# The folded weight W' as three products of rounded terms, and the second batch's turned probabilities copied by ACT

## The chip, the cores and the metric

The kernel runs on one core of a Trainium2 chip. The metric is the device time in microseconds (us) of one execution. PE is the matrix engine, PEld its weight load, DVE the vector engine, ACT the scalar engine, POOL the GpSimd engine, SP the queue that issues most transfers. Each engine works through its own list of instructions in order and waits on semaphores for the others.

## The reference

Three layers follow one another on 2 batches of 768 tokens.

```python
x = attention(q, k, v)                  # 8 heads of 64, a window of 96 and 8 global keys
for e in range(4):                      # attention experts, top 2 of 4 by a gate
    a = softmax(mask(scale * (x @ wq[e]) @ (x @ wk[e]).T))
    ye = a @ (x @ wv[e]) @ wo[e]
    out += gate[:, e] * ye
u = out + transposed(transposed(out) @ U @ V)
y = u + relu(u @ w_ch1) @ w_ch2         # 512 -> 2048 -> 512
```

The kernel never forms `ye` at full width before the first channel product. It keeps the gated expert outputs z (256 wide, 4 experts of 64) and multiplies the stacked `wo` (256x512) into `w_ch1` (512x2048) once: W' = wo @ w_ch1, 256x2048. That product is what the change touches.

## The kernel before, in words

The first part works on 24 pairs of softmax rows: pairs 0 to 11 belong to the first layer, 12 to 17 to the expert attention of batch 0, 18 to 23 to that of batch 1. The code runs over positions; position r computes the scores of pair r + 1 (L485, into PSUM tiles S), the values of pair r - 1 (L774) and the transposes ("turns", L442) of pair r. A pair's way is: PE scores, DVE minima with the mask (L489), ACT exponentials (L500), DVE reciprocal sums (L507 to L510, `rec`), POOL normalisation of the probabilities `pr` (L513), PE transposes into PSUM banks T and U, a copy of each bank to SBUF (`pt`, in `moved`, L289 on ACT for even groups and L292 on DVE for odd ones), PE values. A pair of batch 1 has 3 or 4 groups.

Free room in a position is filled with other products. W' is folded there in 8 slices of 256 columns (`w_fold`): f = 0 in position 15, 1 in 17, 2 in 18, 3 to 5 in 19 to 21, half of 6 in 22; slice 7 and the other half of 6 follow in the tail, behind the last scores. Each slice is 2 row halves times 4 contraction blocks, in plain fp32, which the chip runs as two instructions each: 16 instructions. The slice of `w_ch1` arrives as 64-bit numbers; `w_load` loads it (two raw tiles `cr`), `narrow_sign` (ACT L303, POOL L304) and `narrow_join` (DVE L309, L310) make fp32 tiles `ct` of 128x512 from it, one position ahead of the fold. The result in PSUM (`acc`) is split by `out` into a rounded term (ACT, `wph`) and the remainder (DVE L295, `wpl`), because the later products run on such pairs of terms: `three` multiplies high by high, low by high and high by low in the faster fp32r format (L631, L632). After the tail, the second part (`M`) computes the two channel products in 64 steps, all of it with `three`.

The order of the instructions on each engine is written by a planner (class `Order`) from costs of its own; on PE it keeps the order of the code, on the other engines it moves instructions freely within their dependences.

## Time and profile before

| what | us |
|---|---|
| median of 3 runs (445.39 to 447.91) | 445.65 |
| the profiled execution | 447.32 |
| its span in the profile | 445.2 |
| PE busy in it | 431.1 |
| DVE, ACT, POOL busy in it | 241.6, 194.5, 115.0 |

A busy time says how long an engine was at work, not that it set the end. The span is what the profile covers; 2.1 us of the execution lie outside it. In timelines an instruction's length includes the part that overlaps the next one on the same engine, so what an instruction costs is read from the distance between starts.

### The profile page before, as it was taken

The page shows a single profiled execution, that of the slowest core. Times are in us where ns is not written, and L with a number is a line of the kernel's source. Part 1 is how long each engine was busy: PE and PEld are TensorE (multiplying, and loading weights), DVE is VectorE, ACT ScalarE, POOL GpSimd, SP SyncE. Part 2 cuts the span into 40 slices and gives each one's busy share as a digit, 9 for nine tenths or more (in the row PEclk, how much of TensorE's full clock was granted, in tenths as well). Part 3 has the DMA queues.
Part 4 walks back from the last instruction along what each step waited for, and adds up shares of the span by engine and source line. Part 5 has one row for each costly group of instructions (what it writes and reads, how often), then busy time and mean ns, then how long its engine had stood idle before and what let it go on. Part 6 is the DMA issues. An engine that isn't in the chain of part 4 may idle for free.

```text
span 445.2 us, 9063 instructions
## 1 busy us (share of the span) xinstructions
PE 431.1 (97%) x3444; PEld 373.4 (84%) x3444; DVE 241.6 (54%) x726; ACT 194.5 (44%) x539; POOL 115.0 (26%) x211
## 2 busy tenths in 40 slices
PE   6999999999999999999999999999999999999993
PEld 4777899888888987788888888888888888899993
DVE  6888757885656876987897995111121212221211
ACT  5788676666455556575654652111111111111111
POOL 7756556326232434445221230000000000000000
PEclk9999999999999999999999999999999999999998
DMA  7888853006303123333353422000020000200002
GB/s 262 277 268 274 280 170 77 2 1 237 97 1 96 51 92 113 122 100 104 116 160 112 144 76 73 1 1 0 1 71 0 1 0 1 71 1 0 1 0 78
DMA packets 21733, 39.34 MB, mean 88 GB/s; under 512 B 2802, under 2 KB 7922, under 8 KB 21682
## 3 DMA queue, kind: packets, MB, share of 16 engines
q1 hardware_dynamic: 19952, 37.11, 26.1%
q10 hardware_dynamic: 1730, 1.57, 1.0%
q8 instruction: 29, 0.48, 0.4%
q14 instruction: 22, 0.18, 0.1%
HBM read 35.53 MB, written 3.15 MB: 87 GB/s over the span
## 4 chain that ended last, share of the span: by engine, by line
PE 52%; ACT 0%; ACTq 0%; DVE 0%; issue 0%; DVEq 0%
PE h L631 10%; PE acd L631 8%; PE h L632 5%; PE acc L631 5%; PE X L631 4%; PE acd L632 4%; PE T L631 4%; PE U L631 3%; PE acc L632 2%; PE X L632 2%; PE T L632 2%; PE U L632 1%; PE acc L848 1%; PE S L631 0%; PE X L774 0%; PE T L874 0%
## 5 line engine op out<-in xcount | busy, mean ns | idle before, releaser
L930 DVE SCALAR_TENSOR_TENSOR pr<-h,pr 128x384 fp32r<-128x384 f32 x64 | 35.7, 557 | 133.0 <-ACT pr L929 132.9
L513 POOL TENSOR_SCALAR pr<-pr,rec 128x192 f32<-128x192 f32 (+5 forms) x144 | 76.0, 547 | 96.4 <-DVE rec L510 54.0
L929 ACT ACTIVATE pr<-h 128x384 fp32r<-128x384 f32 x64 | 31.5, 492 | 141.4 <-PE h L632 141.3
L500 ACT ACTIVATE pr<-pr,nm 128x192 f32<-128x192 f32 (+5 forms) x144 | 73.2, 513 | 25.2 <-DVE nm L489 21.0
L304 POOL TENSOR_SCALAR cr<-cr 128x512 f32<-128x512 f32 (+2 forms) x35 | 27.3, 785 | 50.3 <-ACT ct L303 27.0
L848 PE MATMUL acc<-ct,woT 128*128 128x256 f32 x128 | 29.4, 380 | 0.0
L489 DVE CUSTOM_DVE_ANT_0 pr<-S,zT 128x192 f32<-128x192 f32 (+1 forms) x96 | 27.4, 339 | 1.6 <-PE S L541 1.3
L310 DVE SCALAR_TENSOR_TENSOR ct<-ct,cr 128x512 int32<-128x512 int32 (+2 forms) x35 | 27.2, 776 | 0.9
L500 ACT ACTIVATION_READ_ACCUMULATOR pr<-pr,nm 128x1 f32 x144 | 27.5, 191 | 0.0
L489 DVE CUSTOM_DVE_ANT_0 pr<-S,cm 128x512 f32<-128x512 f32 (+3 forms) x48 | 24.7, 552 | 4.2 <-PE S L485 4.0
L309 DVE SCALAR_TENSOR_TENSOR cr<-cr 128x512 int32<-128x512 int32 (+2 forms) x35 | 24.6, 704 | 2.7 <-POOL cr L304 2.6
L848 PEld LDWEIGHTS acc<-ct,woT 128*128 128x128 f32 x128 | 23.5, 190 | 3.0 <-DVE zT L906 0.2
L442 PE MATMUL T<-ident,pr 128*128 128x128 f32 x144 | 24.2, 278 | 1.6 <-POOL pr L513 0.9
L632 PE MATMUL acd<-w2h,pr 128*128 128x512 f32 x64 | 25.4, 396 | 0.0
L631 PE MATMUL acd<-w2l,pr 128*128 128x512 f32 x64 | 25.3, 396 | 0.0
L631 PE MATMUL acd<-w2h,pr 128*128 128x512 f32 x64 | 25.3, 395 | 0.0
L303 ACT ACTIVATE ct<-cr 128x512 f32<-128x512 f32 (+2 forms) x35 | 22.6, 651 | 5.9 <-PE acc L848 5.9
L442 PE MATMUL U<-ident,pr 128*128 128x128 f32 x136 | 23.3, 278 | 0.3
L541 PE MATMUL S<-qk 64*64 64x192 f32 (+1 forms) x384 | 20.0, 346 | 2.3 <-DMA qk<-in_qk_dram 1.7
L485 PE MATMUL S<-qk,qk 64*128 64x512 f32 (+3 forms) x128 | 21.4, 462 | 0.0
L774 PEld LDWEIGHTS X<-pt,v 128*64 128x64 f32 x336 | 18.1, 137 | 3.5 <-issue 2.0
L292 DVE COPY pt<-T 128x384 f32<-128x384 f32 (+1 forms) x26 | 15.8, 608 | 9.6 <-PE T L442 9.3
(290 smaller groups left out, 1043.8 us busy)
## 6 DMA issues: line engine op xcount, KB each, us to landing
cr<-in_w_dram SPq DMA_DIRECT2D x32, 512.0 KB, 3.6
v<-in_vt_dram SPq DMA_DIRECT2D x32, 256.0 KB, 3.9
qk<-in_qk_dram SPq DMA_DIRECT2D x8, 320.0 KB, 3.8
qk<-in_qk_dram SPq DMA_DIRECT2D x8, 272.0 KB, 3.7
qk<-in_qk_dram SPq DMA_DIRECT2D x8, 256.0 KB, 4.2
out_dram<-o SPq DMA_DIRECT2D x12, 128.0 KB, 1.8
out_dram<-o ACTq DMA_DIRECT2D x12, 128.0 KB, 1.9
...
```

The source lines that it names most:

```text
L304: nc.gpsimd.tensor_scalar(hi.bitcast(F32), hi.bitcast(F32), 0.0, -0.0, op0=ALU.mult, op1=ALU.add)
L309: nc.vector.scalar_tensor_tensor(lo, lo, 29, hi, op0=ALU.logical_shift_right, op1=ALU.bitwise_or)
L310: nc.vector.scalar_tensor_tensor(t, t, 3, lo, op0=ALU.logical_shift_left, op1=ALU.bitwise_or)
L442: self.nc.tensor.transpose(t[:, k * P : (k + 1) * P], s, self.ident)
L489: self.nc.vector.tensor_tensor_reduce(out=out, in0=sp, in1=mask, scale=scale, scalar=start, op0=ALU.add, op1=ALU.min, accum_out=nm)
L500: self.nc.scalar.activation(pr[:, h, :], pr[:, h, :], AF.Exp, bias=nm[h], scale=-1.0, accum_out=den[:, k, h : h + 1])
L513: nc.gpsimd.tensor_scalar(pr[:, h, :], pr[:, h, :], rec[:, k - k0, h : h + 1], 0.0, op0=ALU.mult, op1=ALU.add)
L631: mm(out, lh, rh, start=first, stop=False), mm(out, lh, rl, start=False, stop=False),
L632: mm(out, ll, rh, start=False, stop=last)]
L848: nc.tensor.matmul(ac[:, n, :], self.woT[:, kc, p * P : (p + 1) * P], w1[kc // 2][:, kc % 2, :], start=kc == 0, stop=kc == 3)
L929: nc.scalar.activation(hh, hp, AF.Relu)
L930: nc.vector.scalar_tensor_tensor(hl, hp, 0.0, hh.bitcast(F32), op0=ALU.max, op1=ALU.subtract)
```

## The change

W' is folded by `three`. For that `woT` (the transposed `wo`) is loaded into a raw tile instead of a tile of its own, and split by POOL into `woTh` and by DVE into `woTl` (128x1024 each, once). Each `ct` tile is split too: for a slice's first tile ACT rounds, for its second POOL, and DVE subtracts for both (128x512 each). For slices 0 to 4 these terms lie in the columns of `wph` and `wpl` that slices 4 to 7 will fill later; for slices 5 to 7 in new tiles `c`, in a pool `wt2` that opens in position 20. A slice is then 24 fp32r instructions of 128x128 by 128x256. The second edit gives `moved` a flag: for batch 1 the odd groups are copied by ACT as well, 10 copies of 128x512 over positions 18 to 22 and the tail.

```diff
--- before.py
+++ after.py
@@ -441,9 +441,9 @@
         for k, s in enumerate(srcs):
             self.nc.tensor.transpose(t[:, k * P : (k + 1) * P], s, self.ident)
 
-    def moved(self, t, w, g):
+    def moved(self, t, w, g, late=False):
         pt = self.soft_.tile([P, 512], F32, tag=f"pt{g % 2}", name=self.uid("pt"), bufs=2)
-        (self.hi_dve if g % 2 else self.hi_act)(pt[:, :w], t[:, :w])
+        (self.hi_dve if g % 2 and not late else self.hi_act)(pt[:, :w], t[:, :w])
         return pt
 
 
@@ -762,7 +762,7 @@
             us = st["units"]
             t = self.ps("T")
             self.transposes(t, [us[k][0][:, h, kk * P : (kk + 1) * P] for k, kk in groups[g] for h in range(2)])
-            return lambda: st.__setitem__(g, self.moved(t, 2 * P * len(groups[g]), g))
+            return lambda: st.__setitem__(g, self.moved(t, 2 * P * len(groups[g]), g, b == 1))
 
         def values():
             v = self.st[b][2]
@@ -817,9 +817,24 @@
 
     def w_begin(self, wpool, tmp):
         self.wp = [wpool.tile([P, 2, DFF], F32R, name=f"wp{x}") for x in "hl"]
-        self.woT = tmp.tile([P, 4, 2 * P], F32, name="woT")
+        self.woT = [tmp.tile([P, 4, 2 * P], F32R, name=f"woT{x}") for x in "hl"]
         self.w1 = {}
-        self.nc.sync.dma_start(self.woT, self.a["woT"].rearrange("(c r) n -> r c n", r=P))
+
+    def wt_load(self):
+        r = self.raw_tile().bitcast(F32)[:, : 2 * DM].rearrange("p (c n) -> p c n", c=4)
+        self.nc.sync.dma_start(r, self.a["woT"].rearrange("(c r) n -> r c n", r=P))
+        yield
+        self.hi_pool(self.woT[0], r)
+        yield
+        self.lo_dve(self.woT[1], r, self.woT[0])
+        yield
+
+    def w_terms(self, f):
+
+        if f < 5:
+            return [[self.wp[x][:, :, n * CW : (n + 1) * CW] for x in range(2)] for n in ((7, 6) if f % 2 == 0 else (5, 4))]
+        made = [[self.wt2.tile([P, 2, CW], F32R, tag=f"c{x}{n}", name=self.uid("c"), bufs=2) for x in "hl"] for n in range(2)]
+        return made
 
     def w_load(self, f):
         raws, ts = [], []
@@ -830,12 +845,19 @@
             raws.append(raw.rearrange("p (n w) -> p n w", w=2))
         yield
         for r in raws:
-            ts.append(self.wtmp.tile([P, DM], I32, name=self.uid("ct")) if f > 5 else self.narrow_tile())
+            ts.append(self.narrow_tile())
             self.narrow_sign(r, ts[-1])
-        self.w1[f] = [t.bitcast(F32).rearrange("p (c n) -> p c n", c=2) for t in ts]
         yield
         for r, t in zip(raws, ts):
             self.narrow_join(r, t)
+        yield
+        self.w1[f] = terms = self.w_terms(f)
+        ts = [t.bitcast(F32).rearrange("p (c n) -> p c n", c=2) for t in ts]
+        for x, t in enumerate(ts):
+            [self.hi_act, self.hi_pool]["AP"[x] == "P"](terms[x][0], t)
+        yield
+        for t, (h, l) in zip(ts, terms):
+            self.lo_dve(l, t, h)
         yield
 
     def w_fold(self, f, ps=slice(0, 2)):
@@ -845,8 +867,8 @@
         ac = self.bank(self.side).rearrange("p (t n) -> p t n", t=2)[:, ps, :]
         for n, p in enumerate(range(2)[ps]):
             for kc in range(4):
-                nc.tensor.matmul(
-                    ac[:, n, :], self.woT[:, kc, p * P : (p + 1) * P], w1[kc // 2][:, kc % 2, :], start=kc == 0, stop=kc == 3)
+                wh, wl = [w[:, kc, p * P : (p + 1) * P] for w in self.woT]
+                self.three(ac[:, n, :], wh, wl, *[x[:, kc % 2, :] for x in w1[kc // 2]], kc == 0, kc == 3)
         fs = slice(f * CW, (f + 1) * CW)
 
         def out():
@@ -1172,7 +1194,8 @@
         at(11, "mid", self.gate, 0)
         at(17, "mid", self.gate, 1)
         for f, r in enumerate(folds):
-            stages(lambda f=f: self.w_load(f), (r - 2, "dma"), (r - 1, "sign"), (r - 1, "a"))
+            stages(lambda f=f: self.w_load(f), (r - 2, "dma"), (r - 1, "sign"), (r - 1, "a"), (r - 1, "mid"), (r - 1, "end"))
+        stages(self.wt_load, (13, "dma"), (14, "sign"), (14, "mid"))
 
         def middle():
             if not dense:
@@ -1188,6 +1211,7 @@
             self.close(x1p, wpl, stk0)
             self.w2a = self.open("w2a", "right")
             self.wo_tiles(self.w2a)
+            self.wt2 = self.open("wt2", "right")
             for b in range(B):
                 self.y_tiles(b, self.w2a)
 
@@ -1355,7 +1379,7 @@
         for e in ev[1]:
             e()
         do(r + 1, "end")
-        self.close(self.wtmp, self.s1p, self.psumR, self.psumS)
+        self.close(self.wt2, self.wtmp, self.s1p, self.psumR, self.psumS)
         self.psumS = self.open("psumS", space=PSUM)
         self.psumR = self.open("psumR", space=PSUM)
         self.pp = {"h": self.psumS, "acd": self.psumR}
```

On PE the rows of a slice are replaced where they stood, and nothing else moves. This is slice 3 in position 19, with the values of the pair before (X) and the first transposes (U and T are PSUM banks) ahead of it; of the slice's own rows, those of the first half stand here. Before:

```order
L774 MATMUL X_2759<-pt_2732,v_1980 64x128 x4
L774 MATMUL X_2759<-pt_2734,v_1980 64x128 x4
L442 MATMUL U_2809<-ident,pr_2651 128x128 x4
L442 MATMUL T_2814<-ident,pr_2651 128x128 x4
L848 MATMUL acc_2823<-ct_2667,woT 128x256 x2
L848 MATMUL acc_2823<-ct_2670,woT 128x256 x2
```

And now, down to the first contraction block of the slice:

```order
L774 MATMUL X_2827<-pt_2782,v_1980 64x128 x4
L774 MATMUL X_2827<-pt_2784,v_1980 64x128 x4
L442 MATMUL U_2877<-ident,pr_2699 128x128 x4
L442 MATMUL T_2882<-ident,pr_2699 128x128 x4
L631 MATMUL acc_2893<-wph,woTh 128x256
L631 MATMUL acc_2893<-wpl,woTh 128x256
L632 MATMUL acc_2893<-wph,woTl 128x256
```

A row of two instructions has become three rows, and so on for the 8 blocks of the slice: 24 instructions instead of 16.

On DVE the stretch from position 21 into 22 carries the end of pair 22, the term splits of slice 6 and the first minima of pair 23 (`nm`). Before, from the sign joins of slice 6 on:

```order
L309 SCALAR_TENSOR_TENSOR cr_2864<-cr_2864 128x512
L310 SCALAR_TENSOR_TENSOR ct_3011<-ct_3011,cr_2864 128x512
L507 TENSOR_SCALAR rec_3088<-den_2996 128x4
L508 RECIPROCAL rec_3088<-rec_3088 128x4
L510 TENSOR_TENSOR rec_3088<-rec_3088,g_1981 128x4
L292 COPY pt_3061<-U_3054 128x512
L295 TENSOR_TENSOR wpl<-acc_3038,wph 128x2x256
L309 SCALAR_TENSOR_TENSOR cr_2866<-cr_2866 128x512
L310 SCALAR_TENSOR_TENSOR ct_3014<-ct_3014,cr_2866 128x512
L489 ISA pr_3096,nm_3098<-S_3063,cm 128x512
L489 ISA nm_3098 128x1
L292 COPY pt_3133<-U_3126 128x512
```

And now:

```order
L309 SCALAR_TENSOR_TENSOR cr_2955<-cr_2955 128x512
L309 SCALAR_TENSOR_TENSOR cr_2957<-cr_2957 128x512
L310 SCALAR_TENSOR_TENSOR ct_3126<-ct_3126,cr_2955 128x512
L507 TENSOR_SCALAR rec_3227<-den_3111 128x4
L508 RECIPROCAL rec_3227<-rec_3227 128x4
L510 TENSOR_TENSOR rec_3227<-rec_3227,g_1981 128x4
L310 SCALAR_TENSOR_TENSOR ct_3129<-ct_3129,cr_2957 128x512
L295 TENSOR_TENSOR wpl<-acc_3159,wph 128x2x256
L295 TENSOR_TENSOR c_3154<-ct_3126,c_3153 128x512
L295 TENSOR_TENSOR c_3156<-ct_3129,c_3155 128x512
L489 ISA pr_3235,nm_3237<-S_3202,cm 128x512
L489 ISA nm_3237 128x1
```

The copies of `pt` are gone, both joins (L309 to L310) stand close together, and two subtractions of terms (`c`) stand between the remainder of slice 5 (`wpl`) and the first minimum.

On POOL, the stretch from pair 22's normalisation to pair 23's, before:

```order
L513 TENSOR_SCALAR pr_2995<-pr_2995,rec_3088 128x640 x2
L513 TENSOR_SCALAR pr_2995<-pr_2995,rec_3088 128x384 x2
L304 TENSOR_SCALAR cr_2962<-cr_2962 128x512
L304 TENSOR_SCALAR cr_2964<-cr_2964 128x512
L513 TENSOR_SCALAR pr_3096<-pr_3096,rec_3160 128x512 x2
L513 TENSOR_SCALAR pr_3096<-pr_3096,rec_3160 128x128 x2
```

And now:

```order
L513 TENSOR_SCALAR pr_3110<-pr_3110,rec_3227 128x640 x2
L286 TENSOR_SCALAR c_3155<-ct_3129 128x512
L513 TENSOR_SCALAR pr_3110<-pr_3110,rec_3227 128x384 x2
L304 TENSOR_SCALAR cr_3077<-cr_3077 128x512
L304 TENSOR_SCALAR cr_3079<-cr_3079 128x512
L513 TENSOR_SCALAR pr_3235<-pr_3235,rec_3315 128x512 x2
L286 TENSOR_SCALAR c_3276<-ct_3250 128x512
L513 TENSOR_SCALAR pr_3235<-pr_3235,rec_3315 128x128 x2
```

The rounding of slice 6's second tile (`c`, L286) stands between pair 22's two sizes, and that of slice 7's between pair 23's.

On ACT, position 22, where the exponentials of pair 23 (`pr`, L500) lie, before:

```order
L289 ACTIVATE pt_3059<-T_3049 128x512
L289 ACTIVATE wph<-acc_3038 128x2x256
L303 ACTIVATE ct_3111<-cr_2964 128x512
L289 ACTIVATE zT_99<-X_3071 128x2x128
L289 ACTIVATE pt_3131<-T_3121 128x512
L500 ACTIVATE pr_3096,den_3097<-pr_3096,nm_3098 128x512
L500 ACTIVATE pr_3096,den_3097<-pr_3096,nm_3100 128x512
L289 ACTIVATE pt_3152<-T_3142 128x512
L500 ACTIVATE pr_3096,den_3097<-pr_3096,nm_3102 128x128
L500 ACTIVATE pr_3096,den_3097<-pr_3096,nm_3104 128x128
L289 ACTIVATE wph<-acc_3135 128x256
```

And now:

```order
L289 ACTIVATE zT_99<-X_3210 128x2x128
L289 ACTIVATE pt_3270<-T_3260 128x512
L289 ACTIVATE pt_3272<-U_3265 128x512
L500 ACTIVATE pr_3235,den_3236<-pr_3235,nm_3237 128x512
L500 ACTIVATE pr_3235,den_3236<-pr_3235,nm_3241 128x128
L289 ACTIVATE pt_3305<-T_3295 128x512
L303 ACTIVATE ct_3250<-cr_3079 128x512
L289 ACTIVATE pt_3307<-U_3300 128x512
L500 ACTIVATE pr_3235,den_3236<-pr_3235,nm_3239 128x512
L500 ACTIVATE pr_3235,den_3236<-pr_3235,nm_3243 128x128
L289 ACTIVATE c_3274<-ct_3247 128x512
L289 ACTIVATE wph<-acc_3280 128x256
```

Four copies of `pt` stand there instead of two, and the second head's two exponentials come last, behind the third and fourth copy and a sign step of slice 7 (L303).

## Rows read from the trace of the kernel before

**Rows 1.** The page, first part: busy time, share and instructions of each engine.
```profile
PE 431.1 (97%) x3444; PEld 373.4 (84%) x3444; DVE 241.6 (54%) x726; ACT 194.5 (44%) x539; POOL 115.0 (26%) x211
```

**Rows 2.** Positions 20 to 22: length, busy us (count): PE, PEld, DVE, ACT, POOL.
```profile
176.72:185.24 8.52, 8.52 (x72) 6.87 (x71) 7.42 (x22) 6.33 (x15) 2.54 (x5) 1.00 0.22 70
185.24:193.76 8.52, 8.52 (x65) 6.70 (x64) 6.97 (x20) 5.50 (x14) 4.44 (x7) 1.00 0.42 126
193.76:202.46 8.70, 8.70 (x97) 7.35 (x97) 7.43 (x19) 5.52 (x15) 4.46 (x6) 1.00 0.36 117
```

**Rows 3.** PE, position 22 and the tail's beginning: start, us, instructions, idle before.
```profile
193.76 1.35 PE L485 MATMUL S<-qk,qk 64*128 64x512 f32 x8
196.94 0.65 PE L442 MATMUL T<-ident,pr 128*128 128x128 f32 x4
197.87 1.89 PE L848 MATMUL acc<-ct,woT 128*128 128x256 f32 x8
199.60 0.60 PE L442 MATMUL T<-ident,pr 128*128 128x128 f32 x4
...
204.00 0.33 PE L442 MATMUL T<-ident,pr 128*128 128x128 f32 x1
205.10 0.55 PE L442 MATMUL T<-ident,pr 128*128 128x128 f32 x3 [0.77 <-POOL pr L513]
```

**Rows 4.** The chain that ended last, 176 to 207 us: start, us, what.
```profile
205.10 0.55 PE T L442 x3
```

**Rows 5.** Timeline of PE, position 19.
```profile
172.30 3.62 PE L848 MATMUL acc<-ct,woT 128*128 128x256 f32 x16
175.75 0.60 PE L442 MATMUL U<-ident,pr 128*128 128x128 f32 x4
```

**Rows 6.** Timeline of PE, the last block's 128x256 products.
```profile
432.04 0.28 PE L631 MATMUL U<-w2h,pr 128*128 128x256 f32 x1
...
432.75 0.33 PE L631 MATMUL h<-y11h,wph 128*128 128x384 f32 x1
```

**Rows 7.** Groups of instructions on DVE, 127 to 212 us.
```profile
L310 DVE SCALAR_TENSOR_TENSOR ct<-ct,cr 128x512 int32<-128x512 int32 x14 | 11.6, 831 | 0.4
...
L292 DVE COPY pt<-U 128x512 f32<-128x512 f32 x10 | 6.9, 691 | 4.8 <-PE U L442 4.7
L295 DVE TENSOR_TENSOR wpl<-acc,wph 128x512 fp32r<-128x512 f32 x6 | 4.1, 690 | 4.6 <-ACT wph L289 4.5
```

**Rows 8.** Groups of instructions on ACT, the same stretch.
```profile
L303 ACT ACTIVATE ct<-cr 128x512 f32<-128x512 f32 x15 | 9.9, 673 | 5.9 <-PE acc L848 5.9
L289 ACT ACTIVATE pt<-T 128x512 f32<-128x512 f32 x10 | 6.0, 598 | 2.7 <-PE T L442 2.4
```

**Rows 9.** Groups of instructions on POOL, the same stretch.
```profile
L304 POOL TENSOR_SCALAR cr<-cr 128x512 f32<-128x512 f32 x15 | 11.1, 748 | 6.6 <-ACT ct L303 2.7 <-DVE wpl L295 2.2 <-POOL cr L304 1.3
```

**Rows 10.** Timeline of DVE, two places.
```profile
185.05 1.27 DVE L310 SCALAR_TENSOR_TENSOR ct<-ct,cr 128x512 int32<-128x512 int32 x1
...
196.97 0.68 DVE L489 CUSTOM_DVE_ANT_0 pr<-S,cm 128x512 f32<-128x512 f32 x1
```

**Rows 11.** Timeline of ACT, position 22.
```profile
198.19 0.71 ACT L500 ACTIVATE pr<-pr,nm 128x512 f32<-128x512 f32 x1
...
201.17 0.39 ACT L500 ACTIVATE pr<-pr,nm 128x128 f32<-128x128 f32 x1
201.47 0.19 ACT L500 ACTIVATION_READ_ACCUMULATOR pr<-pr,nm 128x1 f32 x1
```

**Rows 12.** Timeline of POOL, three normalises.
```profile
184.57 2.99 POOL L513 TENSOR_SCALAR pr<-pr,rec 128x768 f32<-128x768 f32 x3 [5.65 <-DVE rec L510]
...
193.38 3.13 POOL L513 TENSOR_SCALAR pr<-pr,rec 128x640 f32<-128x640 f32 x4 [4.08 <-DVE rec L510]
...
202.46 3.28 POOL L513 TENSOR_SCALAR pr<-pr,rec 128x512 f32<-128x512 f32 x4 [4.25 <-DVE rec L510]
```

**Rows 13.** The page, fifth part: a weight load of the fold.
```profile
L848 PEld LDWEIGHTS acc<-ct,woT 128*128 128x128 f32 x128 | 23.5, 190 | 3.0 <-DVE zT L906 0.2
```


## The prediction

> **What bounds the kernel now.** I read the page's first part, then the windows by position, then the chain that ended last, then the timelines of the four engines around the one place where PE stands still. PE is at work for 431.1 of 445.2 us [rows 1], and in positions 20 to 22 without a gap: 8.52 of 8.52, 8.52 of 8.52, 8.70 of 8.70 us [rows 2]. So PE sets the time of these positions, and each shorter instruction on it ends the kernel earlier, as long as the others keep up. They are not far behind: DVE is busy 7.42, 6.97 and 7.43 us of the same windows, ACT 6.33, 5.50 and 5.52 [rows 2]. The one gap of PE among the folds lies just behind them. At the tail's beginning the transposes of pair 23, the last pair, start at 204.00, stop, and go on at 205.10 after 0.77 us that are put down to POOL's normalisation [rows 3]. The chain that ended last is PE from that point on [rows 4]. Ahead of 205.10 time is gained by PE only until POOL's result is the later one; behind it everything on PE counts.
>
> **The change part by part.**
>
> *The products.* Slice 3 starts at 172.30 and the transposes behind it at 175.75: 3.45 us for 16 instructions, 0.216 each [rows 5]. The changed slice has 24 fp32r products of 128x128 by 128x256. The last block holds six of these in a row, from 432.04 to 432.75, so 0.118 us each [rows 6], with new weights for each, as the fold has. A slice will take 24 x 0.118 = 2.84 us, 0.61 less, and the eight together 8 x 0.61 = 4.9 us less on PE. I take no extra cost for going from fp32 to fp32r and back: the fold's neighbours of both kinds exist today, and the distance between starts I use includes the one step out of it.
>
> *The splits, per slice.* DVE gets two subtractions of 128x512. The nearest row is today's remainder with one input in PSUM, 0.690 us, and the starts of such instructions stand about 0.61 apart [rows 7]. ACT gets one rounding (a copy of 128x512, 0.598) [rows 8], POOL one (a 128x512 step, 0.748) [rows 9]. For `woT` POOL and DVE get one of 128x1024 each, once, in position 14. Slices 0 to 2 belong to the long positions 15, 17 and 18, with other products beside them, and their splits are done a position ahead; I cost them and `woT` at nothing, because DVE has idle time there: its copies alone wait 4.7 us for PE in that stretch [rows 7]. Without this cover it would be up to 7 x 0.61 = 4.3 us.
>
> *The copies.* Ten copies of 0.691 leave DVE [rows 7] and go to ACT at 0.598 [rows 8]. In positions 19 to 22 DVE gives up one or two and takes two subtractions, so it is where it was or 0.6 higher: at most 7.42 + 0.69 = 8.1 us in position 20. With slices shorter by 0.61 a position has 7.9 us. DVE is then full in position 20, and about 1 us free in 21 and 22 (22 has half a slice and becomes 8.4 long). ACT goes from 6.33 to 7.5 (two more of 0.6) and from 5.5 to 7.3 (three more), still under 7.9. No engine is overrun for long, but their queues leave little room, and the wait moves to the loop of softmax.
>
> *Pair 23, where the end is set.* I follow position 22 from its start, 193.76, in the order of the change. Before: the first minimum starts at 196.97 [rows 10], 3.2 after it; the last exponential is read out at 201.66 [rows 11], 7.9 after; POOL begins at 202.46 and both large heads are done when PE goes on at 205.10, 11.3 after [rows 12, 3]. Now: DVE's second join, the remainder and two subtractions stand ahead of the first minimum, and the second of the subtractions waits for POOL's rounding, which stands behind the two normalisations 128x640. Those are some 1.9 of the 3.13 us of that group [rows 12]. POOL began them 0.4 ahead of the position's start; position 21 is now 0.6 shorter, so it begins 0.3 behind it, the rounding ends about 3.0 after the start and the minima begin at 3.6. That is 0.4 later than before, and as no copy stands among the minima any more they end earlier. The minima are not what is late. On ACT the second head's exponentials now stand behind both copies of the second half. Its transposes began at 199.60, 5.84 after the start [rows 3], 0.31 sooner now by the half slice ahead of them: the first copy can start at 6.0. Copy 0.5, sign step 0.6 and copy 0.5 bring ACT to 7.55, an exponential of 128x512 (0.71) and one of 128x128 (0.39) to 8.65 instead of 7.9 [rows 11]. With the same 0.8 to POOL's start and the same 2.64 for two heads, PE goes on at 12.1 instead of 11.3. So at this place 0.75 us are lost against position 22's start, and the 0.31 that the half slice of position 22 saves is void, because PE waits anyway: together 1.05 us.
>
> *Positions 20 and 21.* The same steps there make pair 21's large normalisations end about 0.2 us ahead of PE, and pair 22's about 0.9. I count 0.2 us for what is lost there in DVE's stretched instructions.
>
> *Behind 205.10.* The slices 7 and the half of 6 in the tail (1.5 slices, 0.9 us of the 4.9) lie on the chain. Their terms are ready: the subtraction that comes last is needed only by the eighth of the first half's 12 products. I take them whole.
>
> *What POOL's work does to DVE's.* The joins have two inputs in SBUF, as the new subtractions have. The mean of the 14 is 0.831 us [rows 7], and the one at 185.05 took 1.27, while POOL was normalising from 184.57 on [rows 10, 12]. If the ten subtractions of slices 3 to 7 stretched as that one did, from 0.69 to 1.27, DVE would have 5.8 us more; I count 0.2 of it. The Trainium skill ("SBUF — State Buffer", section "Who interferes with whom") says that a DVE instruction with two SBUF inputs contends with a GpSimd instruction that reads SBUF, and that whichever comes second is blocked. The trace agrees with that at 185.05. It speaks against this change, which adds 17 such subtractions and 9 POOL instructions; by it the sum would be 3.65 - 5.6 = 2.0 us slower, by the row's mean of the joins it stays near 3.65 faster.
>
> *The sum.* 4.9 - 1.05 - 0.2 = 3.65 us less. The profiled execution would take 447.32 - 3.65 = 443.7; it lies 1.7 us above the median of the three runs, and on the median it is 445.65 - 3.65 = 442.0 us. What the splits cost has no row of its own: the bounds are nothing lost at all (below nothing too, if the lighter DVE ends the 0.77 us wait: 445.65 - 4.9 - 0.8 = 440.0) and the 1.05 with the whole 5.8 us of stretched subtractions (445.65 - 4.9 + 1.05 + 5.8 = 447.6). I take the value near the low end of the loss, because the splits are queued a position ahead of their use.
>
> **The rivals.**
>
> *Everything is hidden.* Pair 23's exponentials come in time, since ACT's copies wait less than I reckon or the minima's lead is kept: 445.65 - 4.9 = 440.8, or 440.0 with the wait gone. For it speaks PE's full windows [rows 2], against it the order of ACT, where the last exponentials can't start before copies that PE releases late.
>
> *The loop of softmax becomes the bound, and the kernel is slower.* In positions 19 to 22 and the tail POOL's rounding stands ahead of or among the normalisations, and it waits for DVE's join, which waits for POOL's own sign step. If each pass through this ring adds a join, a rounding and two subtractions to the pair's way, 0.69 + 0.75 + 1.38 = 2.8 us, and the pair has 1.6 us in hand (pair 22's first two normalisations done at about 195.3, PE's transposes at 196.94) [rows 3, 12], then each of five places loses 1.2, in all 6.0, with the 0.75 of pair 23 on top: 445.65 - 4.9 + 6.75 = 447.5. It decides from 1.6 us of added way per position. Against it: the joins have moved forward in DVE's order, ahead of the `rec` of the next pair, so that most of the ring runs while ACT is at the exponentials.
>
> *The subtractions are stretched.* The same loop, but the price comes from DVE and POOL in each other's way: ten times 0.58 as at 185.05, with pair 23's loss on top, 447.6 [rows 10]. This is where the port's rule ends. For it speaks that DVE is nearly full in position 20; against it that most of today's joins stay near 0.69, or the mean of 14 would not be 0.83 [rows 7].
>
> *The products are no shorter.* If weights had to be loaded with nothing beside them, at 0.19 us each [rows 13], a slice would cost 24 x 0.19 = 4.6 and the kernel 454. The last block's row [rows 6] loads new weights for each product at 0.118 and speaks against it.
>
> **How the numbers follow.** A measurement of this kernel can tell about 1% from no change, 4.5 us: below 441.2 is faster, above 450.1 slower. My forecast, a part of the saving lost at pair 23, has 0.61 and covers 441.2 to 444. Everything hidden has 0.22, 440.0 to 441.2. The softmax loop as bound has 0.08 and the stretched subtractions 0.06, both 444 to 452, where they come together past 450.1 in 0.03. The products no shorter has 0.03. The predicted time is 442.0. The range runs from 440.3 to 446.0: it takes in most of the hidden case and the nearer half of the loop's. Faster by over 1%: 0.23; slower: 0.06; within: 0.71.
>
> **What would show it.** In the profile after, a slice in position 19 should take 2.8 to 2.9 us from its first product to the next transposes. PE's wait for POOL at the transposes of pair 23 should grow from 0.77 to about 1.7 us, with the last exponential some 8.65 us after position 22's scores begin. Positions 19 to 21 should be 7.9 us long, with PE full. The tail from there to the first product of the second part should be about 0.9 us shorter. A wait of PE on a DVE subtraction ahead of a slice, or on POOL in positions 20 to 22, would show the second rival; no wait at pair 23 the first. I am wrong if a product of 256 columns is not near 0.118 us there, or if the splits hold up the normalisations in several positions.

## The result, and the profile after

The changed kernel took 442.65 us (median of 6 runs, 440.27 to 443.47), the kernel before 447.85 beside it (6 runs, 445.39 to 448.72): ratio 0.9897, 95% interval 0.9866 to 0.9928. A second set of 8 runs, on another occasion, gave 443.18 and a ratio of 0.9925 (0.9896 to 0.9954). The medians differ by 5.2 us in the first set and by 3.6 in the second (446.82 before); the intervals stand for 3.2 to 6.0 and 2.1 to 4.6 us. So it is about 1% faster, some 4 us. The profiled execution took 442.87 us with a span of 441.1 (before 447.32 and 445.2).

The page's first part, busy time by engine [rows 1]: PE has 4.7 us less, ACT 8.1 us more, POOL 14.4 us more, DVE 5.6 us more in spite of the ten copies that it gave away.

```profile
PE 426.4 (97%) x3508; PEld 372.9 (85%) x3508; DVE 247.2 (56%) x733; ACT 202.6 (46%) x557; POOL 129.4 (29%) x220
```

The windows of positions 19 to 22 and of the tail up to the first hidden product, with the columns of [rows 2]. Position 20 is 7.89 us long where it was 8.52 and PE is full. Position 21 took 8.15 and position 22 8.55 (8.52 and 8.70 before), and the tail 13.01 us with PE busy for 11.40 of them.

```profile
166.29:174.20 7.91, 7.91 (x82) 6.97 (x81) 3.98 (x15) 5.47 (x15) 3.80 (x5) 1.00 0.23 66
174.20:182.09 7.89, 7.89 (x79) 6.71 (x79) 7.11 (x19) 5.65 (x14) 4.90 (x7) 1.00 0.05 8
182.09:190.24 8.15, 8.15 (x74) 6.62 (x73) 7.20 (x22) 7.42 (x20) 4.73 (x7) 1.00 0.36 125
190.24:198.79 8.55, 8.55 (x101) 7.28 (x100) 6.77 (x18) 7.44 (x18) 5.88 (x7) 1.00 0.46 128
198.79:211.80 13.01, 11.40 (x103) 10.42 (x101) 10.60 (x22) 8.74 (x22) 7.31 (x8) 1.00 0.37 120
```

The timeline of PE in position 19 [rows 5]: slice 3 now runs from 170.32 to 173.23, 2.91 us where it took 3.45. The first product takes 0.20, the other 23 take 0.118 each. The transposes ahead of the slice now take 0.35 us up to its start, where they took 0.44 (171.86 to 172.30), so the first product's 0.08 is made good there.

```profile
169.97 0.60 PE L442 MATMUL T<-ident,pr 128*128 128x128 f32 x4
170.32 0.36 PE L631 MATMUL acc<-wph,woTh 128*128 128x256 f32 x1
170.52 0.28 PE L631 MATMUL acc<-wpl,woTh 128*128 128x256 f32 x1
...
173.23 0.60 PE L442 MATMUL U<-ident,pr 128*128 128x128 f32 x4
```

The timeline of PE at the tail's beginning [rows 3]: the transposes of pair 23 now wait twice for POOL, 1.26 and 0.35 us, where they waited 0.77. From 202.26 to the first hidden product PE is full for 9.54 us.

```profile
198.79 1.53 PE L896 MATMUL S<-ident,zT 128*128 128x128 f32 x12
201.58 0.33 PE L442 MATMUL T<-ident,pr 128*128 128x128 f32 x1 [1.26 <-POOL pr L513]
202.26 0.55 PE L442 MATMUL T<-ident,pr 128*128 128x128 f32 x3 [0.35 <-POOL pr L513]
...
211.80 0.34 PE L631 MATMUL h<-y00h,wph 128*128 128x384 f32 x1
```

The chain that ended last is no longer PE's at this place [rows 4]: from 194.17 on it runs through ACT, over copies, a sign step of slice 7 (`ct`) and pair 23's exponentials.

```profile
195.23 1.20 ACT pr L500 x4
196.47 0.39 ACT pt L289
196.97 0.69 ACT ct L303
197.66 0.49 ACT pt L289
198.15 1.08 ACT pr L500 x4
...
201.51 0.70 POOL pr L513
202.26 0.55 PE T L442 x3
```

From the end of the exponentials to 201.51 the view goes over ACT's rows for other work, but in POOL's own timeline the normalisation of pair 23 fills this time. These are the first minimum of position 22 in DVE's timeline, the read-out of the last exponential in ACT's, and POOL's two normalisations 128x512:

```profile
194.44 0.68 DVE L489 CUSTOM_DVE_ANT_0 pr<-S,cm 128x512 f32<-128x512 f32 x1
...
199.03 0.20 ACT L500 ACTIVATION_READ_ACCUMULATOR pr<-pr,nm 128x1 f32 x1
...
200.04 2.16 POOL L513 TENSOR_SCALAR pr<-pr,rec 128x512 f32<-128x512 f32 x2 [1.60 <-PE S L896]
```

One measure serves for all that follows, **the stretch**: from the first scores of position 15 (121.77 us before, 121.75 after) to the first hidden product (215.35 and 211.80). It holds all products and copies that the change touches. The splits of `woT` and of slice 0 lie ahead of it, in position 14, which is 10.77 us long before and after; the start of the program, which differs between executions, lies outside as well. It took 93.58 us and takes 90.05, 3.53 less. (The first expectations on record name its beginning the first scores of position 13; their 93.58 us shows that position 15 is meant.) By position the saving is 0.62 (15), 0 (16, which folds nothing), 0.64, 0.62, 0.62, 0.63 (17 to 20), 0.37 (21), 0.15 (22), and -0.12 in the tail.

### The profile page after: what moved, and what is told of

It is laid out like the page before. It is cut to its first block, busy times and chain, and to the rows that moved or that the text cites. A ratio compares the mean times of both kernels' runs of the same rounds, so it can differ in the third digit from the quotient of the medians.

```text
span 441.1 us, 9248 instructions
## 1 busy us (share of the span) xinstructions
PE 426.4 (97%) x3508; PEld 372.9 (85%) x3508; DVE 247.2 (56%) x733; ACT 202.6 (46%) x557; POOL 129.4 (29%) x220
## 4 chain that ended last, share of the span: by engine, by line
PE 86%; DMA 9%; ACT 2%; POOL 1%; issue 0%; SPq 0%; ACTq 0%; DVE 0%; DVEq 0%; POOLq 0%
PE acc L631 13%; PE h L631 10%; PE acd L631 8%; PE X L631 7%; PE acc L632 6%; PE h L632 5%; PE S L485 5%; DMA v<-in_vt_dram 4%; PE X L774 4%; PE acd L632 4%; PE T L631 4%; PE X L632 4%; DMA qk<-in_qk_dram 4%; PE T L442 3%; PE U L631 3%; PE U L442 3%
## 5 line engine op out<-in xcount | busy, mean ns | idle before, releaser
L513 POOL TENSOR_SCALAR pr<-pr,rec 128x192 f32<-128x192 f32 (+5 forms) x144 | 82.2, 589 | 70.4 <-DVE rec L510 32.8
L500 ACT ACTIVATE pr<-pr,nm 128x192 f32<-128x192 f32 (+5 forms) x144 | 73.3, 515 | 16.5 <-DVE nm L489 13.3
L304 POOL TENSOR_SCALAR cr<-cr 128x512 f32<-128x512 f32 (+2 forms) x35 | 28.8, 829 | 52.6 <-ACT ct L303 29.1
L500 ACT ACTIVATION_READ_ACCUMULATOR pr<-pr,nm 128x1 f32 x144 | 27.8, 193 | 0.0
L310 DVE SCALAR_TENSOR_TENSOR ct<-ct,cr 128x512 int32<-128x512 int32 (+2 forms) x35 | 25.7, 742 | 0.6
L309 DVE SCALAR_TENSOR_TENSOR cr<-cr 128x512 int32<-128x512 int32 (+2 forms) x35 | 24.1, 696 | 2.4 <-POOL cr L304 2.4
L303 ACT ACTIVATE ct<-cr 128x512 f32<-128x512 f32 (+2 forms) x35 | 22.4, 652 | 0.0
L442 PEld LDWEIGHTS T<-ident,pr 128*128 128x128 f32 x144 | 16.8, 141 | 5.3 <-POOL pr L513 4.1
L289 ACT ACTIVATE pt<-U 128x512 f32<-128x512 f32 (+2 forms) x33 | 16.7, 506 | 10.0 <-PE U L442 9.9
L774 PE MATMUL X<-pt,v 128*64 128x128 f32 x336 | 21.1, 276 | 0.0
```

Source lines behind the costliest of these rows:

```text
L304: nc.gpsimd.tensor_scalar(hi.bitcast(F32), hi.bitcast(F32), 0.0, -0.0, op0=ALU.mult, op1=ALU.add)
L310: nc.vector.scalar_tensor_tensor(t, t, 3, lo, op0=ALU.logical_shift_left, op1=ALU.bitwise_or)
L442: self.nc.tensor.transpose(t[:, k * P : (k + 1) * P], s, self.ident)
L500: self.nc.scalar.activation(pr[:, h, :], pr[:, h, :], AF.Exp, bias=nm[h], scale=-1.0, accum_out=den[:, k, h : h + 1])
L513: nc.gpsimd.tensor_scalar(pr[:, h, :], pr[:, h, :], rec[:, k - k0, h : h + 1], 0.0, op0=ALU.mult, op1=ALU.add)
L774: self.nc.tensor.matmul(zp[h * D : (h + 1) * D, (1 - k) * P : (2 - k) * P], v[:, kk, e * D : (e + 1) * D], st[g][:, (2 * n + h) * P : (2 * ...
```

## The experiments

Stretches are from one profiled execution each; "second" is the time to the second group of hidden products, which shows what was given back just behind the stretch. "Waits" are PE's on another engine's work between position 21 and that group. The ratio is to the kernel before, run beside each kernel on the same chip (its medians there were 446.5 to 447.9), with its 95% interval; it isn't the quotient of the two medians.

| kernel | median us (runs) | ratio | stretch | second | waits us |
|---|---|---|---|---|---|
| before | 447.85 (6) | 1 | 93.58 | 99.52 | 0.77 |
| changed | 442.65 (6) | 0.9897 (0.9866 to 0.9928) | 90.05 | 95.78 | 1.26, 0.35 |
| changed, again | 443.18 (8) | 0.9925 (0.9896 to 0.9954) | 90.04 | 95.79 | 1.26, 0.34 |
| products only | 446.85 (12) | 0.9992 (0.9964 to 1.0019) | 92.65 | 98.40 | 1.01, 0.96, 1.36, 0.77 |
| copies only | 445.35 (12) | 0.9968 (0.9942 to 0.9993) | 92.47 | 98.39 | none |
| fp32 fold, splits, copies | 446.04 (9) | 0.9986 (0.9962 to 1.0011) | 92.73 | 99.05 | 0.30 |
| two products | 440.48 (4) | 0.9835 (0.9788 to 0.9881) | 88.40 | 94.13 | 0.63, 0.17, 0.72, 0.95, 1.41, 0.77 |
| no low terms | 444.47 (4) | 0.9930 (0.9902 to 0.9957) | 90.51 | 96.24 | 1.14, 0.77 |
| pair 22's copies on DVE | 442.75 (6) | 0.9893 (0.9856 to 0.9929) | 89.91 | 95.66 | 0.97, 0.66 |
| one copy on DVE | 443.75 (6) | 0.9922 (0.9895 to 0.9950) | 91.53 | 97.26 | 1.38, 0.35 |
| roundings on POOL | 442.61 (6) | 0.9899 (0.9877 to 0.9920) | 89.87 | 95.60 | 1.26, 0.34 |
| half folds exchanged | 443.01 (11) | 0.9925 (0.9898 to 0.9952) | 88.93 | 95.33 | 0.34, 0.61 |
| exchanged, written later | 442.11 (6) | 0.9903 (0.9875 to 0.9931) | 88.92 | 95.31 | 0.34, 0.61 |
| exchanged, Wo held back | 443.73 (9) | 0.9922 (0.9893 to 0.9951) | 89.39 | 95.98 | 0.34, 0.19, 0.79 |

**The change without its second edit.**

```diff
-        (self.hi_dve if g % 2 and not late else self.hi_act)(pt[:, :w], t[:, :w])
+        (self.hi_dve if g % 2 else self.hi_act)(pt[:, :w], t[:, :w])
```

> The change without its second edit: DVE copies the odd groups of batch 1 as before. Measure: the front part, from the first scores of position 13 to the first product of the second part (93.58 us before, 90.05 changed), and PE's waits at pair 23's transposes (0.77 before, 1.61 changed). Theory (PE's shorter products give 4.9 us, ACT's order at pair 23 takes some back): pair 23's exponentials no longer stand behind two copies, the wait is 1.0 or less, front part 89.3 to 90.1, ratio to before 0.987 to 0.991. Rival (the gain hangs on the copies, because DVE can't hold splits and copies): DVE has 8.4 to 8.8 us of work in positions of 7.9, each of 19 to 22 loses 0.5 to 0.9, front part 92 to 93.6, ratio 0.995 to 1.0.

Of the 3.53 us only 0.93 are left, the rival's case by its numbers, but not by its places. The scores of position 22 still start as early as in the changed kernel (68.48 us after those of position 15, there 68.49), so up to position 21 the shorter slices are all there, where the rival had each position from 19 on lose 0.5 us or more. Behind that the timeline of PE has four waits:

```profile
195.57 0.33 PE L442 MATMUL T<-ident,pr 128*128 128x128 f32 x1 [1.01 <-POOL pr L513]
196.85 0.55 PE L442 MATMUL T<-ident,pr 128*128 128x128 f32 x3 [0.96 <-POOL pr L513]
...
202.52 1.09 PE L774 MATMUL X<-pt,v 128*64 128x128 f32 x16 [1.36 <-ACT pt L289]
205.96 0.55 PE L442 MATMUL T<-ident,pr 128*128 128x128 f32 x3 [0.77 <-POOL pr L513]
```

With its copies DVE doesn't do the splits in time in position 22. Its first minimum of position 22 (scores at 191.32) starts at 198.63, 7.3 us after them, where the changed kernel has 4.2.

**The second edit alone**, in the kernel before.

```diff
-        (self.hi_dve if g % 2 else self.hi_act)(pt[:, :w], t[:, :w])
+        (self.hi_dve if g % 2 and not late else self.hi_act)(pt[:, :w], t[:, :w])
...
-            return lambda: st.__setitem__(g, self.moved(t, 2 * P * len(groups[g]), g))
+            return lambda: st.__setitem__(g, self.moved(t, 2 * P * len(groups[g]), g, b == 1))
```

> The kernel before with the second edit alone: fp32 products, no splits, ACT copies all groups of batch 1. Theory: no gain of its own, front part 93.6 to 94.4 (93.58 before), since PE's instructions are the same and ACT's copies can only delay pair 23's exponentials; ratio 1.000 to 1.002. Rival (the copies bring a part of the gain by relieving DVE): PE's wait at pair 23 goes from 0.77 to nothing, front part 92.8, ratio 0.998.

The rival's case, and a little more: the stretch is 1.11 us shorter. The 0.77 us wait of [rows 3] is gone and no other came; by the distances between starts these transposes had cost 0.18 us ahead of the first and 0.93 behind it. In PE's timeline the transposes of pair 23 run through:

```profile
203.01 0.71 PE L442 MATMUL T<-ident,pr 128*128 128x128 f32 x4
203.56 0.60 PE L442 MATMUL U<-ident,pr 128*128 128x128 f32 x4
203.99 1.89 PE L848 MATMUL acc<-ct,woT 128*128 128x256 f32 x8
```

The two edits alone give 0.93 + 1.11 = 2.04 us, together 3.53: the two together give 1.5 us more than one by one.

**The splits without the shorter products.** The fold multiplies fp32 as before, ACT has the copies, the slices are split (`woT` is not) and nobody reads the terms. Of the edit this is the product; the rest loads `woT` as before and keeps the `ct` tiles for it.

```diff
-                wh, wl = [w[:, kc, p * P : (p + 1) * P] for w in self.woT]
-                self.three(ac[:, n, :], wh, wl, *[x[:, kc % 2, :] for x in w1[kc // 2]], kc == 0, kc == 3)
+                nc.tensor.matmul(
+                    ac[:, n, :], self.woF[:, kc, p * P : (p + 1) * P], self.ct[f][kc // 2][:, kc % 2, :], start=kc == 0, stop=kc == 3)
...
```

> The fold multiplies by fp32 as before, ACT copies the second batch's odd groups as in the changed kernel, and the splits of the slices are made as in the changed kernel but nobody reads them: their load without the shorter products. With the copies alone the stretch from the first scores of position 15 to the first hidden product took 92.47 us. Theory (the splits load engines that have room until position 20, and cost only in positions 21 to 23): 0.3 to 1.0 us on top, 92.8 to 93.5, with a wait at pair 23 of 0.3 to 1 us. Rival (the fp32 products leave so much room on TensorE's side that the splits are hidden throughout): 92.3 to 92.7 and no wait at pair 23.

The rival's case: 92.73 against 92.47 with the copies alone, and no wait at pair 23. While PE needs 3.45 us a slice, the splits are hidden. What holds pair 23 in the changed kernel is thus not the splits alone; that it is the shorter positions is argued, since the order differs too. Here the second sign step of slice 7 stands behind the last exponential (201.62 against 200.76), which begins 7.03 us after the scores of position 22 (193.73), and POOL's two normalisations take 1.36 us together. To the second group it costs 0.66, of which 0.30 is a wait for `y00l`.

**Two products for three.** The product of the low `woT` with the high slice is left out, so its share is missing from the result.

```diff
-                self.three(ac[:, n, :], wh, wl, *[x[:, kc % 2, :] for x in w1[kc // 2]], kc == 0, kc == 3)
+                rh, rl = [x[:, kc % 2, :] for x in w1[kc // 2]]
+                nc.tensor.matmul(ac[:, n, :], wh, rh, start=kc == 0, stop=False)
+                nc.tensor.matmul(ac[:, n, :], wh, rl, start=False, stop=kc == 3)
```

> The change with two products instead of three: the low term of wo times the high term of the slice is left out, so a part of W' is missing. PE has 64 x 0.118 = 7.6 us less than the change. Theory (PE sets the time up to pair 23, whose loop is nearly closed): slices 0 to 2 and those of the tail give their 2.8 and 1.4 us, slices 3 to 6 give little of their 3.3, because pair 21 to 23's normalisations have 0.2 to 0.9 us in hand: front part 84.5 to 86, PE waits for POOL in two or more positions. Rival (PE alone is the bound, with room to spare): all 7.6 come out, front part 82.5.

PE has 8 x 8 x 0.118 = 7.6 us less to do, and 1.65 come out. At 88.40 us the stretch is longer than the theory had it (84.5 to 86), let alone the rival (82.5). Positions 15 and 17 to 20 are 0.94 to 0.97 shorter each than in the changed kernel, as eight products are, 4.7 in all, and so slices 3 and 4 give the whole of what the theory held to be mostly lost. From position 21 on 3.1 us of it are lost again: that one is 8.25 us long (changed: 8.15), position 22 10.44 (8.55). Its windows, up to the first hidden product; the last column but two is the granted clock:

```profile
177.64:185.89 8.25, 7.45 (x65) 5.70 (x64) 7.00 (x21) 6.80 (x17) 5.97 (x7) 1.00 0.41 129
185.89:196.33 10.44, 8.65 (x98) 6.87 (x97) 8.46 (x21) 8.26 (x22) 6.39 (x7) 1.00 0.33 102
...
200.36:204.00 3.64, 3.64 (x18) 3.57 (x19) 1.18 (x2) 1.01 (x3) 1.66 (x3) 0.53 0.18 72
```

The waits of PE there are on POOL's normalised probabilities but for 0.17 on DVE: behind position 20 the softmax loop is the bound, and a faster fold gives nothing more. Of the 3.1 us some 1.7 (an estimate, 3.64 x 0.47) went to the clock, of which more below; without it 3.35 of the 7.6 would have come out.

**No low terms.** DVE's subtractions for the slices are left out; the second product takes the high term again, so the low terms of W1 are missing from the result.

```diff
-        for t, (h, l) in zip(ts, terms):
-            self.lo_dve(l, t, h)
...
-                self.three(ac[:, n, :], wh, wl, *[x[:, kc % 2, :] for x in w1[kc // 2]], kc == 0, kc == 3)
+                self.three(ac[:, n, :], wh, wl, *[w1[kc // 2][0][:, kc % 2, :]] * 2, kc == 0, kc == 3)
```

> The low terms of the folded slices are not made (sixteen 128x512 subtractions less on DVE, 0.76 to 1.04 us each in the changed kernel's trace); the second product of each three takes the high term instead, so W1's low terms are missing from the result and TensorE's products are the same. The stretch from the first scores of position 15 to the first hidden product took 93.58 us before and 90.05 in the changed kernel, which still waits 1.61 us for POOL's normalised probabilities at pair 23 and runs positions 21 and 22 at 8.15 and 8.55 us instead of 7.9. Theory (the softmax loop of the last positions is held by the sum of what DVE, POOL and ACT do, DVE's subtractions included, which also stretch POOL's rows): most of 0.25 + 0.65 + 1.6 us comes back, the stretch is 88.0 to 89.0. Rival (ACT's order alone holds it, DVE's work is hidden): the wait stays over 1.2 us, the stretch is 89.6 to 90.1.

The theory falls: DVE is rid of sixteen subtractions, position 21 is 7.94 long instead of 8.15, and yet the waits are 1.91 us and the stretch is 90.51, above the rival's 89.6 to 90.1 as well. The timeline of ACT in position 22 (scores at 192.73) shows where the time went. The copy of pair 22's turned probabilities comes at 197.40 and the sign step of slice 7 stands among the exponentials, so that the last of these begins 8.71 us after the scores (8.50 in the changed kernel), although the first minimum begins 3.34 after them (4.20).

```profile
200.18 0.72 ACT L500 ACTIVATE pr<-pr,nm 128x512 f32<-128x512 f32 x1
...
200.89 0.66 ACT L303 ACTIVATE ct<-cr 128x512 f32<-128x512 f32 x1
201.44 0.40 ACT L500 ACTIVATE pr<-pr,nm 128x128 f32<-128x128 f32 x1
```

Taking the subtractions away thus doesn't shorten the waits. That they are hidden in the changed kernel isn't shown by it, because the order changed with them: a join of slice 7 (1.06 us from 203.47) now stands beside POOL's two normalisations of pair 23, which take 2.07. (This kernel's time of 444.47 us is not comparable: 2.7 us of the profiled execution went ahead of position 15, and the window from 40 to 60 us, where the edit has nothing yet, shows a mean clock of 0.91 with PE busy for 18.62 of 20 us, against 1.00 and 19.85 in the changed kernel. PE stood there for 1.15 us for POOL, at 47.84, ahead of the fall; why this wait came stays open.)

**Pair 22's copies back on DVE**, both of them, and **one of them**.

```diff
-            return lambda: st.__setitem__(g, self.moved(t, 2 * P * len(groups[g]), g, b == 1))
+            return lambda: st.__setitem__(g, self.moved(t, 2 * P * len(groups[g]), g, b == 1 and (p, n) != (1, 1)))
```

> The change, but pair 22's odd groups, whose copies lie in position 22, are copied by DVE; in ACT's list pair 23's four exponentials then stand together, ahead of the copies of the second half. Theory (ACT's order sets pair 23): the last exponential is read out about 8.2 us after position 22's start instead of 8.99, PE's waits there fall from 1.61 to 0.8 to 1.0, front part 89.3 to 89.5 (90.05 changed). Rival (the splits set it, by POOL's rounding ahead of DVE's subtraction and the late minima): the waits stay at 1.4 to 1.8 and the front part at 89.9 to 90.2, or get longer, since DVE has two copies more.

With both on DVE the wait at pair 23 falls to 0.66, but 0.97 us appear at pair 22's values, in front of it. The sum is 1.63 instead of 1.61. The theory's first step holds, its last doesn't. The last exponential begins 7.54 us after the scores (190.09), 0.96 sooner. But in DVE's timeline two of slice 7's join steps now stand among pair 23's reciprocals, the last of which begins 9.43 us after the scores (9.44 in the changed kernel), and PE goes on 11.90 after them (12.02). These are two rows of PE and, between them, that reciprocal of DVE:

```profile
198.66 1.09 PE L774 MATMUL X<-pt,v 128*64 128x128 f32 x16 [0.97 <-ACT pt L289]
...
199.52 0.16 DVE L510 TENSOR_TENSOR rec<-rec,g 128x4 f32<-128x4 f32 x1
...
201.99 0.55 PE L442 MATMUL T<-ident,pr 128*128 128x128 f32 x3 [0.66 <-POOL pr L513]
```

For one copy the condition reads `b == 1 and ((p, n) != (1, 1) or g != 1)`.

> The changed kernel, with one of the two odd copies of the pair in position 22 back on DVE (with both back, the wait at pair 23 fell from 1.61 to 0.66 us but one of 0.97 came at pair 22's values; the stretch was 89.91 against 90.05). Theory (work in position 22 is about equal on ACT and DVE, so any split gives the same): stretch 89.7 to 90.1. Rival (one copy is the balance that neither engine waits for): 89.2 to 89.6, with under 1.0 us of waits in both places together.

The waits are 1.38 and 0.35, so nothing is balanced by it. The stretch is 91.53, 1.48 us longer than the changed kernel's, and neither the theory nor the rival had that. It lies behind the wait: from 200.77 to the first hidden product PE took 11.08 us for what took 9.54. With 9.54 the stretch would be 89.99, the theory's case (an estimate). The windows of 1 us show its clock:

```profile
201.00:202.00 1.00, 1.00 (x10) 1.00 (x9) 0.66 (x1) 0.58 (x2) 1.00 (x3) 0.82 0.84 258
202.00:203.00 1.00, 1.00 (x6) 1.00 (x6) 1.00 (x3) 0.78 (x3) 1.00 (x2) 0.50 0.42 168
203.00:204.00 1.00, 1.00 (x7) 1.00 (x6) 0.99 (x2) 0.00 (x0) 0.46 (x1) 0.50 0.01 4
204.00:205.00 1.00, 1.00 (x7) 0.78 (x7) 0.23 (x1) 0.65 (x2) 0.00 (x0) 0.50 0.00 0
205.00:206.00 1.00, 1.00 (x10) 0.94 (x9) 1.00 (x2) 0.30 (x1) 0.61 (x1) 0.97 0.00 0
```

**Both roundings of slices 6 and 7 on POOL**, one of each being ACT's.

```diff
-            [self.hi_act, self.hi_pool]["AP"[x] == "P"](terms[x][0], t)
+            [self.hi_act, self.hi_pool][("AP" if f < 6 else "PP")[x] == "P"](terms[x][0], t)
```

> The changed kernel, with both roundings of the last two folded slices on POOL (one of each was ACT's). ACT loses two rows of 0.6 to 0.7 us in positions 21 and 22, POOL gets two of 0.7 to 1.04 us. Theory (ACT's sum of copies, roundings and exponentials in position 22 sets the last exponential): the last exponential comes 0.6 us earlier, the wait of 1.61 us at pair 23 falls to about 1.0, the stretch of 90.05 us is 89.4 to 89.7. Rival (POOL has no room either: its normalisations stand behind the added roundings): the wait stays or grows, 90.0 to 91.0.

The first half of the theory holds: the last exponential begins 7.91 us after position 22's scores (190.95), 0.59 sooner. The second doesn't: the waits are unchanged. In DVE's timeline the order has moved slice 7's second join ahead of pair 23's reciprocals, which waited for it; the last of them begins 9.81 us after the scores (9.44 in the changed kernel):

```profile
199.52 0.91 DVE L310 SCALAR_TENSOR_TENSOR ct<-ct,cr 128x512 int32<-128x512 int32 x1
200.36 0.16 DVE L507 TENSOR_SCALAR rec<-den 128x4 f32<-128x4 f32 x1
...
200.76 0.16 DVE L510 TENSOR_TENSOR rec<-rec,g 128x4 f32<-128x4 f32 x1
```

So it is not one engine's queue: slice 7's steps stand among pair 23's on ACT and on DVE, and moving one brings the other forward.

**The half folds exchanged.** In the tail the first half of slice 6, whose terms have been ready since position 22, takes the place of slice 7's, which comes last. Slice 7's terms are then wanted 3.7 us later, and the order puts its work behind pair 23's on both engines.

```diff
-        self.w_fold(7, slice(0, 1))()
+        self.w_fold(6, slice(0, 1))()
...
-        self.w_fold(6, slice(0, 1))()
+        self.w_fold(7, slice(0, 1))()
```

> The changed kernel with two half folds of the tail exchanged: the first half of slice 6, whose terms are ready, stands where the first half of slice 7 stood, and slice 7's comes last, so slice 7's terms are wanted 3.7 us later and its joins, roundings and subtractions fall behind pair 23's exponentials and reciprocals on ACT and DVE. In the changed kernel the last exponential began 8.5 us after position 22 did, the reciprocals were ready at 9.6 us, and TensorE waited 1.26 and 0.35 us for POOL's normalised probabilities; the stretch from the first scores of position 15 to the first hidden product was 90.05 us. Theory (what holds pair 23 is the work of slice 7 in ACT's and DVE's queues ahead of it; moving both together, unlike the runs that moved one): the last exponential 0.6 us earlier, the waits together 0.4 to 1.0 us, the stretch 89.0 to 89.6, the kernel 0.5 to 1 us faster than the changed one. Rival (the pair's own chain of minimum, exponential, normalisation and transposition sets it): the waits stay over 1.3 us and the stretch over 89.8.

The theory's case, by more than it expected: of 1.61 us of waits 0.34 is left, and the stretch is 88.93, 1.12 us shorter than the changed kernel's. The last exponential begins 7.91 us after position 22's scores (190.05), POOL begins at 199.26, and its two normalisations 128x512 take 1.36 together (2.16 in the changed kernel, beside the end of slice 7's second join and its first subtraction). PE goes on 10.62 us after the scores where it was 12.02: of the 1.40, 0.59 come from the exponentials and 0.80 from the normalisations. But DVE now has slice 7's work in the tail, and puts the subtraction for Wo between the two `y00l`. The first line is POOL's, the second PE's at pair 23, then DVE's at the end of the stretch, then PE's wait for it:

```profile
199.26 1.36 POOL L513 TENSOR_SCALAR pr<-pr,rec 128x512 f32<-128x512 f32 x2 [3.33 <-PE S L896]
...
200.67 0.55 PE L442 MATMUL T<-ident,pr 128*128 128x128 f32 x3 [0.34 <-POOL pr L513]
...
210.24 1.22 DVE L295 TENSOR_TENSOR wol<-cr,woh 128x1024 fp32r<-128x1024 f32 x1
211.37 0.55 DVE L295 TENSOR_TENSOR y00l<-zT,y00h 128x384 fp32r<-128x384 f32 x1
...
211.98 0.44 PE L631 MATMUL h<-y00l,wph 128*128 128x384 f32 x1 [0.61 <-DVE y00l L295]
```

To the second group 0.45 us are left, which the times can't tell from nothing.

**The exchange, with slice 7's stages also written half a position later.**

```diff
-            stages(lambda f=f: self.w_load(f), (r - 2, "dma"), (r - 1, "sign"), (r - 1, "a"), (r - 1, "mid"), (r - 1, "end"))
+            stages(lambda f=f: self.w_load(f), *(((r - 2, "dma"), (r - 1, "sign"), (r - 1, "a"), (r - 1, "mid"), (r - 1, "end")) if f < 7 else ((21, "dma"), (22, "mid"), (22, "end"), (23, "mid"), (23, "mid"))))
```

> As the exchange of the half folds, and slice 7's own stages are written half a position later, which also changes which tiles of the rotating buffers they take. Theory: like the exchange alone within 0.3 us, 89.0 to 89.6 from the first scores of position 15 to the first hidden product, since the order of the work comes from when it is wanted. Rival: the later place moves slice 7's subtractions behind the fold that wants them, a wait for DVE's term appears at slice 7's first half fold, 0.3 to 1.0 us slower than the exchange alone.

The same within 0.02 us in both measures: the order comes from when the terms are wanted, as the theory had it.

**The exchange, with Wo's subtraction held behind the second `y00l`.**

```diff
-        stages(self.wo_load, (22, "end"), (23, "mid"), (23, "end"))
+        stages(self.wo_load, (22, "end"), (23, "mid"), (23, "end2"))
...
+        self.hold(lambda: do(r, "end2"), "DVE")
```

> The exchange of the half folds with one thing more: the subtraction that makes Wo's low term (128x1024, 1.21 us on DVE) is held behind the second y00l. With the exchange alone the stretch from the first scores of position 15 to the first hidden product fell from 90.05 to 88.93 us, but DVE had put Wo's subtraction between the two y00l, and TensorE waited 0.61 us for the second; to the second group of hidden products it was 95.33 us against 95.78 in the changed kernel. Theory (that place is the whole of what was given back): no wait for y00l, 94.6 to 94.9 us to the second group, 0.9 to 1.2 us less than the changed kernel. Rival (DVE's work of the tail is then late for the first output products, which want Wo's low term): a wait of 0.4 us or more there, 95.2 us or more.

The rival's case. The wait for `y00l` is gone, and PE waits 0.79 us (and 0.19 earlier) a few products later, at the first output product, as DVE's last remainder now stands behind Wo's subtraction, stretched to 1.67:

```profile
210.57 1.67 DVE L295 TENSOR_TENSOR wol<-cr,woh 128x1024 fp32r<-128x1024 f32 x1
212.16 0.41 DVE L295 TENSOR_TENSOR wpl<-acc,wph 128x256 fp32r<-128x256 f32 x1
...
212.62 0.49 PE L631 MATMUL acc<-woh,y00h 128*128 128x512 f32 x1 [0.79 <-DVE wpl L295]
```

**The changed kernel beside it**, unaltered.

> The changed kernel unaltered, to stand beside the exchange with Wo's subtraction held back on the same chip and in the same rounds. Both theories: 95.7 to 95.9 us from the first scores of position 15 to the second group of hidden products, and 0.5 to 1.3 us slower than the other by the first theory, within 0.5 us of it by the rival.

Its stretch repeats within 0.01 us. None of the variants that compute the whole is measurably faster than it: what the exchange wins at pair 23 is given back where DVE's work of the tail (slice 7's terms, `y00l`, Wo) is wanted.

## Why the prediction was right, point by point

442.0 us was forecast, 442.65 came. The sum of the steps was 3.65 us, the stretch shows 3.53 and the time to the second group of hidden products 3.74. That the time itself came so near has luck in it: its base was 445.65 us, the median of three, and the six runs beside the changed kernel have 447.85.

- **The products** (24 x 0.118, 0.61 less per slice): right. Positions 15 and 17 to 20 are 0.62 to 0.64 shorter, PE full. The case of products no shorter is out. The step between fp32 and fp32r was taken at nothing, and by the position it is nothing: 0.08 us at the first product (170.32 to 170.52) against 0.09 less ahead of it.
- **The splits and `woT` at nothing up to position 20**: right. DVE's idle time was named as the cover. The products alone show that it is there even with the copies still on DVE, up to position 21; from position 22 on it isn't. The fp32 fold with splits shows that under longer slices the load is hidden even at pair 23. DVE was thought full in position 20 at 8.1 us; it is busy for 7.11 of 7.89 there.
- **Positions 20 and 21, 0.2 us**: 0 and 0.24.
- **Pair 23, 1.05 us lost**: the size was right, by two errors that cancel, and its cause half right. The waits are 1.61 us where about 1.7 was foretold, and PE goes on 12.02 us after the scores, where 12.1 was. Position 22 and the tail save 0.15 - 0.12 = 0.03 us, where their two slices should have given 1.2. The prediction put the loss down to two copies and a sign step ahead of the exponentials on ACT. The last exponential is read out 8.99 us after the scores (8.65 foretold), 0.34 later; POOL's two normalisations took 2.16 (2.64 foretold, as before), 0.48 less. The copies alone are not the cause: with them on DVE the sum of the waits stayed at 1.63. The exchange of the half folds took 1.27 us of the waits away, with all copies still on ACT. What was missing is the rest of slice 7's own work, its joins and subtractions on DVE: they run beside pair 23's normalisations in the changed kernel, and stand among its reciprocals where ACT is relieved. The 2.64 held such company without saying so; without it they take 1.36.
- **The minima "begin at 3.6"**: mis-sized, 4.2. POOL's rounding began 2.52 us after the scores instead of about 2.25 and took 1.04 instead of 0.75, and DVE's subtraction waited 0.51 for it. It cost 0.1 us at most: in ACT's list two copies stand ahead of the first exponential, and the second of them began 0.57 us ahead of it (194.66 to 195.23), where ACT's copies in a row stand 0.5 apart.
- **Behind the wait, 0.9 us**: right. Up to the first hidden product 0.71 are there (9.54 against 10.25), and 0.19 more lie just behind it: the second hidden product follows after 0.18 us (211.80 to 211.98), where it was 0.37 behind the fp32 fold (215.35 to 215.72).
- **POOL's work in DVE's way, 0.2 us**: right in size for DVE. The groups from 110 to 208 us, mean ns behind the count and busy time, show the subtractions with two SBUF inputs at 862 and 785 ns where the one with an input in PSUM takes 689, so 0.15 each, not the 0.58 of 185.05 [rows 10]:

```profile
L295 DVE TENSOR_TENSOR wpl<-ct,wph 128x512 fp32r<-128x512 f32 x10 | 8.3, 862 | 0.5 <-POOL wph L286 0.5
L295 DVE TENSOR_TENSOR c<-ct,c 128x512 fp32r<-128x512 f32 x6 | 4.7, 785 | 2.0 <-POOL c L286 2.0
L295 DVE TENSOR_TENSOR wpl<-acc,wph 128x512 fp32r<-128x512 f32 x6 | 4.1, 689 | 0.8 <-ACT wph L289 0.7
```

The rule of the Trainium skill ("SBUF — State Buffer", section "Who interferes with whom") that the later of the two is blocked agrees with single rows (1.11 us for a subtraction beside a normalisation and the rounding behind it, 2.16 for two normalisations that took 1.36 without company). As a price on DVE's subtractions the 5.8 us were far too high. The prediction looked at DVE alone; where the company counts is POOL, whose 0.80 us at pair 23 lie on PE's way.

Of the rivals, the softmax loop as bound is a matter of degree: it doesn't decide at three products, but one product less brings it on, from position 21.
